# A bias that comes to all partitions by DMA instead of GpSimd's broadcast, a first weight load as a step of its own, and a new order of steps

## The chip, the cores and the metric

The kernel runs on one core of a Trainium2 chip. The metric is device microseconds of one execution; the median of several runs counts. The profile is one further execution, taken by the hardware profiler.

## The reference

Attention with rotary embedding over 4 batches, 8 heads, 576 positions and a head dimension of 64, then two layers of mixture of experts over the 2304 tokens of 512 elements. In the first layer a bias is added to the routing logits by the token's modality; the change touches how this bias gets to the chip.

```python
attn = softmax(rotate(q) @ rotate(k).T / sqrt(64)) @ v        # per batch and head
x = attn as [2304, 512]
# first layer: 8 experts, each token goes to one
logits = x @ w_gate + modality_bias[modality_id]              # [2304, 8]
e = argmax(logits); g = softmax(logits)[e]
x = g * (relu(x @ w1[e]) @ w2[e])
# second layer: only tokens with x @ w_skip > 0
x = x + g2 * (relu(x @ w1_2[e2]) @ w2_2[e2])
```

## The kernel before

**The attention** goes over 16 pairs of heads (p = 0 to 15, four pairs to a batch). Each pair is cut into some 100 small steps, which are Python functions in `attention` (L268 to L681): `load` (q, k, v by SP), `rope0` and `rope1` (the rotation of q and of k, L321; VectorE for the first pair, GpSimd for the others), `qk_tr`, `qk_hi`, `qk_lo` (transposition on TensorE into PSUM, and the split into a high and a low part on ScalarE and VectorE), `stackq`, `stackk`, `stack2` (ten moves from SBUF to SBUF by SP's queue, L401 to L423, that put the parts into the layouts that the score matmuls want), `s_mm`, `s_max`, `s_exp` (scores, maximum, exponential), `t_mm`, `t_hi`, `t_lo` (transposes of the exponentials), `pv` (the product with v, whose split is `v_hi` on ScalarE and `v_lo` on GpSimd), `o_ev`, `o_mm`, `o_norm` (output transposition L577, division by the sums, and the routing logits), and `x_store` (L586: three DMAs, of 256 KB and twice 16 KB, of the pair's output to the output tensor).

`s_mm0a` to `s_mm3b` take the scores of 128 rows each; `s_mm4` takes the last 64 rows of both heads. The "a" half reads what `stackq` and `stackk` move, `s_mm4` also what `stack2` moves.

**The order** is written out by hand. Every step has a place in the table POS; pair p's step stands at 10 * p + POS, steps outside the pairs stand at base 0, 110 (what follows the twelfth pair) or 150. All steps are sorted by place, and each engine and each DMA queue gets its instructions in that order (L609 to L681). So only the order between steps of one engine matters, not the numbers themselves. Engines wait for each other by semaphores.

**Around the change.** `constants1` (L223) has SP load small tables, among them the bias as one row of 16 numbers in `mbr`. `constants2` (L236) has GpSimd spread it over 128 partitions with `partition_broadcast` into `mbb`, and convert the modality ids. `constants3` (VectorE) and `constants4` (GpSimd) make `bias1` from it, which `route1` adds to the logits of a batch. `constants6` (L259) has SP load the second gate and fill the two lists in DRAM with void entries (L265). `route1` to `route4p` are the routing of a batch, mostly on GpSimd; `scat0` to `scat4` are indirect DMAs that write token numbers into the list (L807). After the twelfth pair `ahead1` counts tokens of three batches and picks the first expert, `ahead2` has SP load that expert's w1 into `raw1` (L1018, four pieces of 512 KB) and GpSimd load the first two parts of the list (L947), and `ahead3` makes token numbers of them (L1042) and gathers their rows (L951). `moe1_load2` loads w2 into `raw2`, which shares its memory with rope's tiles (`mem_w`). `x_mm0` and `x_mm1` (L1073) transpose the gathered rows, `m_mm` (L1094) multiplies with w1. `warm1` to `warm3` are dummy transposes (L600).

The expert layers behind the attention take blocks of 256 and of 128 tokens in a list order that the data decide; nothing in them is edited.

Of the kernel before, what the change touches and what calls it, by code (L numbers as in the profile page):

```python
# [10 lines left out]
F32 = mybir.dt.float32  # L11
# [11 lines left out]
N, DM, E, F = 2304, 512, 8, 1024  # L23
# [13 lines left out]


POS = dict(
    load=-36.7017, rope0=-33.9451, rope1=-30.111, v_hi=-21.4821, v_lo=-18.1897,  # L40
    qk_tr0=(-30.6061, -30.6042, -30.5936, -30.1223), qk_tr1=(-28.4904, -28.4904, -28.4848, -28.4848),
    qk_tr2=(-29.2463, -29.2463), qk_hi0=-29.4052, qk_hi1=-27.2491, qk_hi2=-29.202, qk_lo0=-29.1934, qk_lo1=-26.9027,
    qk_lo2=-28.9941, stackq=-25.8754, stackk=-23.011, stack2=-22.5711,
    s_mm0a=(-22.0577, -22.0577, -22.0577, -22.0577), s_max0a=-21.4825, s_exp0a=-20.8972,
    s_mm1a=(-21.3076, -21.3076, -21.3076, -21.3076), s_max1a=-20.1346, s_exp1a=-19.5976,
    s_mm2a=(-22.2316, -22.2316, -22.2316, -22.2316), s_max2a=-21.7162, s_exp2a=-21.4126,
    s_mm3a=(-20.5225, -20.5225, -20.5225, -20.5225), s_max3a=-19.2489, s_exp3a=-17.295,
    s_mm0b=(-14.3536, -14.1043, -14.0042, -13.9921), s_max0b=-12.9587, s_exp0b=-12.9046,
    s_mm1b=(-13.0069, -12.9105, -12.9105, -12.9105), s_max1b=-12.8704, s_exp1b=-12.8563,
    s_mm2b=(-15.4526, -15.4526, -15.4386, -15.4386), s_max2b=-14.6158, s_exp2b=-14.0784,  # L50
    s_mm3b=(-16.5055, -16.5055, -16.5055, -16.5055), s_max3b=-15.336, s_exp3b=-15.2119,
    s_mm4=(-19.1859, -19.1807, -19.1807, -19.1807, -19.1807, -19.1807, -19.1807, -19.1331), s_max4=-17.2632,
    s_exp4=-16.1016, l_mma=(-12.7178, -12.6968, -12.6968, -12.6968, -12.6968), l_hia=-12.6823, l_loa=-12.3966,
    t_mm0a=(-12.9092, -12.9092, -12.9092, -12.9092), t_hi0a=-12.8887, t_lo0a=-12.6464,
    pv0a=(-12.6813, -12.3155, -12.1921, -12.051), t_mm1a=(-14.662, -14.3587, -14.3361, -14.0627), t_hi1a=-14.0257,
    t_lo1a=-12.9105, pv1a=(-11.482, -10.94, -10.9025, -10.9025), t_mm2a=(-16.3817, -16.3207, -16.3207, -16.3207),
    t_hi2a=-15.4958, t_lo2a=-15.2606, pv2a=(-12.0718, -11.7295, -11.7295, -11.7295),
    t_mm3a=(-16.0635, -15.4829, -15.3061, -15.3061), t_hi3a=-14.423, t_lo3a=-14.3448,
    pv3a=(-11.6779, -11.4985, -11.4827, -11.4827), pv4a=(-10.0997, -9.6192), o_eva=-8.4242,
    o_mma=(-3.8821, -3.1843, -3.04, -3.0069, -3.0069), o_norma=-2.9092,  # L60
    l_mmb=(-12.5752, -12.5752, -12.5752, -12.5752, -12.5752), l_hib=-12.3276, l_lob=-12.2073,
    t_mm0b=(-12.4134, -12.3969, -12.3818, -12.3818), t_hi0b=-12.2316, t_lo0b=-11.9973,
    pv0b=(-6.7017, -6.7017, -6.7017, -6.5129), t_mm1b=(-7.8953, -7.8953, -7.8953, -7.4024), t_hi1b=-6.7199,
    t_lo1b=-6.1978, pv1b=(-5.2632, -4.5696, -3.9061, -3.5847), t_mm2b=(-11.6405, -11.6405, -11.6405, -11.6405),
    t_hi2b=-11.3076, t_lo2b=-11.3076, pv2b=(-6.5077, -6.5077, -6.2903, -6.172),
    t_mm3b=(-10.8705, -10.8705, -10.8705, -10.8705), t_hi3b=-9.8594, t_lo3b=-9.5279,
    pv3b=(-5.2659, -5.2659, -5.2659, -5.2659), pv4b=(-3.1789, -3.0274), o_evb=-3.008,
    o_mmb=(-2.908, -2.9041, -2.9041, -2.8421, -2.8421), o_normb=-2.5794,
    t_mm4=(-12.3715, -12.3715, -12.3715, -12.3715), t_hi4=-11.4863, t_lo4=-11.4473, r_inv=-4.0473, x_store=-1.9435,
    route1=-0.138, route2=22.2105, route2a=0.0711, route2b=2.3991, route2c=5.809, route2d=6.9931, route2e=3.0369,  # L70
    route2p=7.9451, route3=10.8285, route4=11.1643, route4p=13.5564, scat0=15.9086, scat1=17.0957, scat2=21.6619,
    scat3=22.8497, scat4=24.3127, ahead1=20.7865, ahead2=24.8061, ahead3=26.173, load2=-9.6073, w_hi0=-4.399,
    w_lo0=-2.8576, w_hi1=-10.8843, w_lo1=-10.3037, w_hi2=-3.048, w_lo2=429.3001, w_hi3=-3.3916, w_lo3=-3.1985,
    x_mm0=-2.5275, x_hi0=-2.4128, x_lo0=-2.2031, x_mm1=-2.35, x_hi1=-2.1246, x_lo1=-2.0387, m_mm0=48.2393,
    m_hi0=181.3328, m_lo0=1552.441, m_mm1=611.0564, m_hi1=1628.6892, m_lo1=1629.4085, m_mm2=1553.3863, m_hi2=1625.391,
    m_lo2=1629.4891, m_mm3=6.3202, m_hi3=25.9681, m_lo3=44.977, route1z=0.3768, route2z=49.5846, route2pz=83.0433,
    route3z=164.2886, route4z=197.8744, route4pz=247.5439, scat0z=1554.3317, scat1z=1556.1501, scat2z=1556.8609,
    scat3z=1626.076, scat4z=1629.4488, w2_hi0=3.7676, w2_lo0=6.9592, w2_hi1=0.3352, w2_lo1=2.9321, w2_hi2=-0.7596,
# [34 lines left out]
class Kernel:  # L113
# [154 lines left out]
    def attention(self):  # L268

        nc, wp, pp, rp = self.nc, self.wp, self.pp, self.rp  # L270
# [353 lines left out]
        for p in range(NPAIR):  # L624
# [903 lines left out]
```

## Time and profile before

| | us |
|---|---|
| median of three runs (769.36 to 770.71) | 769.93 |
| profiled execution, its own time | 767.88 |
| its span, from first to last instruction | 766.2 |
| TensorE busy | 725.8 (95%) |
| VectorE, ScalarE, GpSimd busy | 504.0, 435.3, 359.4 |

The mean granted clock of TensorE is 0.975 of full speed. Full speed is 2.4 GHz; the other level is 1.2 GHz. The profiled execution's own time lies 2.05 us below the median of the runs, and its span 1.68 us below its own time.

In the rows, PE is TensorE, DVE VectorE, ACT ScalarE, POOL GpSimd, SP the engine that issues most DMAs; a q behind the name is the engine's sequencer. An arrow names what ended a wait.

### The profile page before, as it was taken

How to read it: one execution, taken by the hardware profiler on the slowest of the kernel's cores; microseconds unless marked ns; L12 is line 12 of the kernel's file. 1: busy time of each engine (PE TensorE's matmuls, PEld its weight loads, DVE VectorE, ACT ScalarE, POOL GpSimd, SP SyncE). 2: the span in 40 equal slices, each digit the busy share in tenths (PEclk: the TensorE clock that was granted, in tenths of full speed). 3: DMA queues.
4: the chain of work that ended last, by engine and by line, in shares of the span. 5: the costliest groups of instructions: out<-in, count | busy, mean ns of one | idle time of the engine just before them, and what ended most of it. 6: DMA issues, size and time to landing. Idle time of an engine off the chain costs nothing. (4 is left out here: it accounts for less than half of the span.)

```text
span 766.2 us, 15348 instructions
## 1 busy us (share of the span) xinstructions
PE 725.8 (95%) x4948; PEld 654.8 (85%) x4948; DVE 504.0 (66%) x1216; ACT 435.3 (57%) x940; POOL 359.4 (47%) x498
## 2 busy tenths in 40 slices
PE   7898999999999999979899999999999979999994
PEld 6797999999999999968799989988998868877773
DVE  6786899988898899984433333323446753589892
ACT  3785888888888888871222222222235542388781
POOL 7728548767876785253343323231434512133233
PEclk8898999999999999999999999999999989999998
DMA  4654554655465544460011101211693301669910
GB/s 139 137 136 121 136 131 120 148 134 134 119 149 131 137 118 102 118 221 1 15 57 42 42 29 49 51 33 38 178 338 146 124 6 40 242 247 316 325 48 20
DMA packets 75199, 92.29 MB, mean 120 GB/s; under 512 B 29440, under 2 KB 50176, under 8 KB 75090
## 3 DMA queue, kind: packets, MB, share of 16 engines
q1 hardware_dynamic: 65938, 73.74, 34.4%
q0 software_dynamic: 7200, 12.46, 5.2%
q10 hardware_dynamic: 1952, 4.85, 2.1%
q8 instruction: 43, 0.70, 0.4%
q14 instruction: 66, 0.54, 0.3%
HBM read 62.11 MB, written 12.95 MB: 98 GB/s over the span
## 5 line engine op out<-in xcount | busy, mean ns | idle before, releaser
L430 PE MATMUL S<-w1s 128*128 128x288 f32 x640 | 124.8, 321 | 3.0 <-DVE w1s L398 1.2
L1143 PE MATMUL psY<-w2s,hT 128*128 128x512 f32 x480 | 119.3, 397 | 0.0
L1094 PE MATMUL psM<-xT,w1s 128*128 128x256 f32 x864 | 112.6, 287 | 0.0
L1094 PEld LDWEIGHTS psM<-xT,w1s 128*128 128x128 f32 x864 | 106.8, 191 | 0.6 <-issue 0.6
L430 PEld LDWEIGHTS S<-w1s 128*128 128x128 f32 x640 | 95.9, 195 | 6.7 <-ACT PP L447 1.6
L1143 PEld LDWEIGHTS psY<-w2s,hT 128*128 128x128 f32 x480 | 87.2, 188 | 16.7
L447 ACT ACTIVATE PP<-S,nm 128x576 f32<-128x576 f32 x128 | 95.8, 748 | 8.0 <-DVE nm L443 7.5
L443 DVE TENSOR_REDUCE nm<-S 128x1 f32<-128x576 f32 x128 | 94.7, 750 | 3.4 <-PE S L430 3.4
L532 DVE TENSOR_TENSOR tl<-T,th 128x512 fp32r<-128x512 f32 x128 | 88.0, 687 | 11.8 <-ACT th L528 8.7
L525 PE MATMUL T<-ident,PP 128*128 128x128 f32 x512 | 87.4, 275 | 1.1 <-DVE w1s L399 0.4
L528 ACT CAST th<-T 128x512 fp32r<-128x512 f32 x128 | 74.8, 584 | 17.5 <-PE T L525 14.9
L559 PE MATMUL O<-th,vh 128*128 128x288 f32 x256 | 74.0, 329 | 0.6 <-ACT os L568 0.5
L1107 DVE SCALAR_TENSOR_TENSOR hT<-psM,hT 128x512 fp32r<-128x512 f32 x36 | 24.9, 690 | 68.6 <-ACT hT L1102 57.8
L1407 PE MATMUL psY<-w2s,hT 128*128 128x512 f32 x240 | 63.8, 403 | 4.3 <-DVE hT L1386 4.3
L1367 PE MATMUL psM<-w1s,xT 128*128 128x512 f32 x240 | 62.4, 408 | 4.5 <-DVEq L1290 4.5
L525 PEld LDWEIGHTS T<-ident,PP 128*128 128x128 f32 x512 | 63.1, 141 | 3.6 <-DVE tl L532 0.8
L1102 ACT ACTIVATE hT<-psM 128x512 fp32r<-128x512 f32 x36 | 21.5, 598 | 74.1 <-PE psM L1094 73.6
L559 PE MATMUL O<-tl,vh 128*128 128x288 f32 x256 | 61.7, 306 | 0.0
L961 POOL DMA_INDIRECT list<-tg,si x20 | 20.2, 1008 | 85.7 <-issue 56.2
L1367 PEld LDWEIGHTS psM<-w1s,xT 128*128 128x128 f32 x240 | 45.0, 193 | 14.7 <-ACTq L1290 4.6
L1407 PEld LDWEIGHTS psY<-w2s,hT 128*128 128x128 f32 x240 | 43.0, 188 | 15.3 <-DVE hT L1386 6.9
L330 POOL TENSOR_TENSOR mem_w<-qkn,mem_w 128x640 f32<-128x640 f32 x30 | 47.0, 1568 | 19.1 <-PE T L367 11.9
(263 smaller groups left out, 1413.9 us busy)
## 6 DMA issues: line engine op xcount, KB each, us to landing
raw<-in_moe_w_dram SPq DMA_DIRECT2D x20, 512.0 KB
mem_w<-in_moe_w_dram SPq DMA_DIRECT2D x20, 512.0 KB
w1s<-w1s SPq DMA_DIRECT2D x30, 256.0 KB
raw1b<-in_moe_w_dram SPq DMA_DIRECT2D x12, 512.0 KB
raw2b<-in_moe_w_dram SPq DMA_DIRECT2D x12, 512.0 KB
w1s<-w1s SPq DMA_DIRECT2D x16, 288.0 KB
qkn<-in_q_dram SPq DMA_DIRECT2D x16, 256.0 KB
qkn<-in_k_dram SPq DMA_DIRECT2D x16, 256.0 KB
```

The source lines that it names most:

```text
L330: eng.tensor_tensor(r, x, tb[:, i, 0].unsqueeze(1).broadcast_to([128, 2, 5, D]), op=ALU.mult)
L430: yield nc.tensor.matmul(ps[:, hf, 0:288], s["wide"][:, o : o + 128], s["K"][h % 2][:, kk, hf * 288 : hf * 288 + 288], start=first and kk ...
L443: nc.vector.tensor_reduce(st[h // 2]["nm"][:, h % 2, c : c + 1], hs[h]["ps", c][:, :, 0:288], axis=AX.XY, op=ALU.max, negate=True)
L447: nc.scalar.activation(PP[:, c, h % 2 * S : h % 2 * S + S].rearrange("p (a b) -> p a b", a=2), hs[h]["ps", c][:, :, 0:288], AF.Exp, bias=s ...
L525: yield nc.tensor.transpose(ps[:, c * 128 : c * 128 + 128], PP[:, c, o : o + 128], ident)
L528: nc.scalar.copy(hs[h]["th"][:, j, 0:512], hs[h]["tp", j])
L532: nc.vector.tensor_tensor(s["tl"][:, j, 0:512], s["tp", j], s["th"][:, j, 0:512].bitcast(F32), op=ALU.subtract)
L559: yield nc.tensor.matmul(s["ot"][:, hf, 0:288], st[h // 2]["vh"][:, h % 2, j].rearrange("p s d -> p (s d)"), w[:, hf * 288 : hf * 288 + 28 ...
L1094: self.nc.tensor.matmul(ps[:, a], self.w1s[:, wi, dc, fs], x[:, xi, dc], start=(dc == 0 and wi + xi == 0), stop=(dc == 3 and wi == 1))
L1143: nc.tensor.matmul(ps, h[:, hi, f, t * 128 : t * 128 + 128], w2s[:, wi, f], start=(f == 0 and hi + wi == 0), stop=(f == 7 and hi == 1))
L1367: nc.tensor.matmul(ms[hf], x[:, xi, dc], w1s[:, wi, dc, hf * 512 : hf * 512 + 512], start=(dc == 0 and wi + xi == 0), stop=(dc == 3 and xi ...
L1407: nc.tensor.matmul(y, hT[:, hi, f], w2s[:, wi, f], start=(f == 0 and hi + wi == 0), stop=(f == 7 and hi == 1))
```

## The change

The bias is loaded into all 128 partitions by the DMA that brought one row before, and the broadcast goes. The load of the first expert's w1 is taken out of `ahead2` and gets a place of its own. All places in POS are new; most of a pair's steps move by about 7 together, which changes nothing between them. Of the table only the lines with steps that are spoken of below stand here.

```diff
-    load=-36.7017, rope0=-33.9451, rope1=-30.111, v_hi=-21.4821, v_lo=-18.1897,
+    load=-40.2545, rope0=-39.1031, rope1=-38.1966, v_hi=-28.3147, v_lo=-23.8684,
...
-    qk_lo2=-28.9941, stackq=-25.8754, stackk=-23.011, stack2=-22.5711,
+    qk_lo2=-35.4693, stackq=-30.1381, stackk=-30.0982, stack2=-25.509,
...
-    t_mm4=(-12.3715, -12.3715, -12.3715, -12.3715), t_hi4=-11.4863, t_lo4=-11.4473, r_inv=-4.0473, x_store=-1.9435,
-    route1=-0.138, route2=22.2105, route2a=0.0711, route2b=2.3991, route2c=5.809, route2d=6.9931, route2e=3.0369,
+    t_mm4=(-19.6242, -19.6242, -19.6242, -19.6242), t_hi4=-18.9706, t_lo4=-17.4754, r_inv=-11.2088, x_store=1.9574,
+    route1=-6.9814, route2=22.2105, route2a=-4.1901, route2b=-1.229, route2c=0.1453, route2d=4.0619, route2e=-0.6407,
...
-    scat3=22.8497, scat4=24.3127, ahead1=20.7865, ahead2=24.8061, ahead3=26.173, load2=-9.6073, w_hi0=-4.399,
+    scat3=16.9444, scat4=19.5742, ahead1=14.2223, ahead2=19.7233, ahead3=29.4759, load1=14.5742, load2=-24.2645,
...
-    x_mm0=-2.5275, x_hi0=-2.4128, x_lo0=-2.2031, x_mm1=-2.35, x_hi1=-2.1246, x_lo1=-2.0387, m_mm0=48.2393,
+    w_lo3=-10.9597, x_mm0=-8.6121, x_hi0=-8.4037, x_lo0=-8.2937, x_mm1=-9.9397, x_hi1=-8.6978, x_lo1=-8.5079,
...
-    w2_hi6=5.4516, w2_lo6=35.4726, w2_hi7=-0.1195, w2_lo7=1.6545, const1=-11.4827, const6=-0.4859, const2=-2.0544,
-    const3=21.5765, const4=22.9241, const5=-41.9989, warm1=-42.8466, warm2=-28.4242, warm3=-36.7926, warm4=1629.4689,
+    w2_hi5=-6.1284, w2_lo5=11.6538, w2_hi6=-9.6901, w2_lo6=-8.8372, w2_hi7=-10.1036, w2_lo7=11.0842, const1=-19.7718,
+    const6=29.8505, const2=-1.1138, const3=13.7753, const4=21.8754, const5=-41.303, warm1=-41.3244, warm2=-27.378,
...
-        self.mbr = self.wp.tile([1, 2, E], F32, name="mbr", bufs=1)
-        nc.sync.dma_start(self.mbr, self.mb.unsqueeze(0))
+        self.mbb = self.wp.tile([128, 2, E], F32, name="mbb", bufs=1)
+        nc.sync.dma_start(self.mbb, self.mb.unsqueeze(0).broadcast_to([128, 2, E]))
...
     def constants2(self):
 
         nc, cp = self.nc, self.cp
-        self.mbb = self.wp.tile([128, 2, E], F32, name="mbb", bufs=1)
-        nc.gpsimd.partition_broadcast(self.mbb, self.mbr)
         self.mf = self.wp.tile([128, B * 5], F32, name="mf", bufs=1)
...
                 for i, f in enumerate((self.moe1_ahead1, self.moe1_ahead2, self.moe1_ahead3)):
                     at(10 * p, f"ahead{i + 1}", f)
+                at(10 * p, "load1", self.moe1_load1)
...
-    def moe1_ahead2(self):
+    def moe1_load1(self):
         q = self.q1
         q.e = self.reg(q.first["meta"][0:1, 0:1], [ET.SP], E - 1)
         self.load(self.raw1, q.w[0], q.e)
+
+    def moe1_ahead2(self):
+        q = self.q1
         for i in range(NA1):
             self.seq_list(q, i)
```

What the sorted table gives for each queue, where it differs:

- SP before: load, stackq, stackk, stack2, x_store (of two pairs back) and again. After: load, stackq, stackk, x_store (of three pairs back), stack2. constants6 stood between the first x_store and the fifth load; it now stands between the eighth load and the seventh pair's stackq. constants1 now stands ahead of the second pair's stack2. At the end, before: the stores of the 13th and 14th pair, w1, the 15th pair's store, w2, the last store; after: the 13th pair's store, w1, w2, the last three stores.
- GpSimd before: rope0 of the fourth pair, constants2, rope1, v_lo; after: rope0, rope1, v_lo, constants2. rope1 now comes ahead of route1 and of route2d.
- TensorE: warm2 stood ahead of the first score matmuls s_mm2a of the first pair and now stands behind s_mm1a, ahead of s_mm3a. x_mm1 comes ahead of x_mm0. Some transposes and matmuls of a pair change places.
- VectorE and ScalarE: the order within a pair stays; small routing steps and the order of the weight splits at the end change.

## Rows read from the trace of the kernel before

**Rows 1.** Windows: busy us (count) of each engine, clock, DMA share, GB/s.
```profile
60.00:80.00 20.00, 16.22 (x111) 15.56 (x111) 11.97 (x27) 11.46 (x29) 14.88 (x13) 0.83 0.46 113
80.00:100.00 20.00, 20.00 (x161) 19.05 (x160) 18.00 (x36) 17.23 (x41) 11.10 (x9) 1.00 0.54 135
```

**Rows 2.** TensorE's timeline in the attention: start us, us, what, idle time before.
```profile
42.33 0.60 PE L364 MATMUL T<-ident,mem_w 128*128 128x128 f32 x4
...
48.10 0.34 PE L577 MATMUL T<-IIg,os 128*128 128x72 f32 x2
...
64.07 0.37 PE L367 MATMUL T<-ident,mem_w 64*128 64x64 f32 x1 [3.78 <-POOL mem_w L336]
...
73.80 0.34 PE L577 MATMUL T<-IIg,os 128*128 128x72 f32 x2
...
150.44 0.34 PE L577 MATMUL T<-IIg,os 128*128 128x72 f32 x2
...
181.73 1.32 PE L430 MATMUL S<-w1s 128*128 128x288 f32 x8
```

**Rows 3.** GpSimd's timeline around constants2.
```profile
44.56 1.57 POOL L336 TENSOR_TENSOR mem_w<-mem_w 128x640 f32<-128x640 f32 x1
51.94 0.29 POOL L240 PARTITION_BROADCAST mbb<-mbr  x1 [5.81 <-issue]
...
59.23 1.54 POOL L330 TENSOR_TENSOR mem_w<-qkn,mem_w 128x640 f32<-128x640 f32 x1 [6.84 <-PE T L525]
```

**Rows 4.** Instructions of lines 240 and 330: ns min/median/max, first to last start.
```profile
L240 POOLq MODIFY_POOL_CONFIG  x2: 15/15/15, 46.1 to 46.1; - x2
...
L330 POOLq MODIFY_POOL_CONFIG  x2: 102/102/102, 52.3 to 52.4; - x2
```

**Rows 5.** SP's timeline: constants6's void stores, and one steady pair.
```profile
55.67 1.96 SPq L265 DMA_DIRECT2D list<-void  x2
...
163.92 9.93 SPq L402 DMA_DIRECT2D w1s<-w1s  x10
...
174.60 2.28 SPq L592 DMA_DIRECT2D out_dram<-xb  x2
```

**Rows 6.** TensorE's timeline at the start.
```profile
14.59 1.35 PE L600 MATMUL O<-ident 128*128 128x128 f32 x8
...
21.81 0.84 PE L364 MATMUL T<-ident,mem_w 128*128 128x128 f32 x3
22.30 1.31 PE L430 MATMUL S<-w1s 128*128 128x288 f32 x4
```

**Rows 7.** SP's timeline: the first expert's w1 and w2.
```profile
318.78 2.34 SPq L1018 DMA_DIRECT2D raw<-in_moe_w_dram  x4
...
330.67 2.20 SPq L1018 DMA_DIRECT2D mem_w<-in_moe_w_dram  x4
```

**Rows 8.** GpSimd's timeline at the hand-over.
```profile
319.30 0.93 POOL L807 DMA_INDIRECT list<-g_tg,g_si  x1 [2.93 <-DVE nm L464]
326.49 0.79 POOL L947 DMA_DIRECT2D list<-list  x1 [6.27 <-DMA list<-g_tg,g_si]
...
330.50 0.18 POOL L1042 CAST tok<-list 128x2 int32<-128x2 f32 x1 [2.30 <-DMA list<-list]
...
332.78 1.48 POOL L951 DMA_INDIRECT xg<-out_dram,tok  x1 [0.30 <-issue]
```

**Rows 9.** TensorE's timeline at the hand-over.
```profile
341.32 0.63 PE L1073 MATMUL T<-ident,xg 128*128 128x128 f32 x4 [1.45 <-DMA xg<-out_dram,tok]
...
343.35 7.17 PE L1094 MATMUL S<-xT,w1s 128*128 128x256 f32 x47 [0.32 <-DVE xT L1080]
...
352.09 3.12 PE L1094 MATMUL S<-xT,w1s 128*128 128x256 f32 x24
```

**Rows 10.** Windows: two us beside the first load (columns as in rows 1).
```profile
324.00:326.00 2.00, 2.00 (x20) 2.00 (x18) 1.62 (x4) 1.83 (x4) 0.00 (x0) 1.00 1.04 414
```

**Rows 11.** DMA issues: out<-in, queue, count, median us to landing.
```profile
xg<-out_dram,tok POOLq DMA_INDIRECT x22, 4.0
```

More of the change, by code (lines that the diff above doesn't have):

```diff
@@ L39 @@
 POS = dict(
-    load=-36.7017, rope0=-33.9451, rope1=-30.111, v_hi=-21.4821, v_lo=-18.1897,
-    qk_tr0=(-30.6061, -30.6042, -30.5936, -30.1223), qk_tr1=(-28.4904, -28.4904, -28.4848, -28.4848),
-    qk_tr2=(-29.2463, -29.2463), qk_hi0=-29.4052, qk_hi1=-27.2491, qk_hi2=-29.202, qk_lo0=-29.1934, qk_lo1=-26.9027,
-    qk_lo2=-28.9941, stackq=-25.8754, stackk=-23.011, stack2=-22.5711,
-    s_mm0a=(-22.0577, -22.0577, -22.0577, -22.0577), s_max0a=-21.4825, s_exp0a=-20.8972,
-    s_mm1a=(-21.3076, -21.3076, -21.3076, -21.3076), s_max1a=-20.1346, s_exp1a=-19.5976,
@@ L46 @@
[L46 to L68, printed above, removed]
@@ L69 @@
-    t_mm4=(-12.3715, -12.3715, -12.3715, -12.3715), t_hi4=-11.4863, t_lo4=-11.4473, r_inv=-4.0473, x_store=-1.9435,
-    route1=-0.138, route2=22.2105, route2a=0.0711, route2b=2.3991, route2c=5.809, route2d=6.9931, route2e=3.0369,
-    route2p=7.9451, route3=10.8285, route4=11.1643, route4p=13.5564, scat0=15.9086, scat1=17.0957, scat2=21.6619,
-    scat3=22.8497, scat4=24.3127, ahead1=20.7865, ahead2=24.8061, ahead3=26.173, load2=-9.6073, w_hi0=-4.399,
-    w_lo0=-2.8576, w_hi1=-10.8843, w_lo1=-10.3037, w_hi2=-3.048, w_lo2=429.3001, w_hi3=-3.3916, w_lo3=-3.1985,
@@ L74 @@
-    x_mm0=-2.5275, x_hi0=-2.4128, x_lo0=-2.2031, x_mm1=-2.35, x_hi1=-2.1246, x_lo1=-2.0387, m_mm0=48.2393,
[L75 to L78, printed above, removed]
@@ L79 @@
-    w2_lo2=-0.5096, w2_hi3=-2.8008, w2_lo3=-0.4501, w2_hi4=4.8596, w2_lo4=46.894, w2_hi5=-2.8731, w2_lo5=-2.4756,
-    w2_hi6=5.4516, w2_lo6=35.4726, w2_hi7=-0.1195, w2_lo7=1.6545, const1=-11.4827, const6=-0.4859, const2=-2.0544,
-    const3=21.5765, const4=22.9241, const5=-41.9989, warm1=-42.8466, warm2=-28.4242, warm3=-36.7926, warm4=1629.4689,
-    switch=-2.9023,
+    load=-40.2545, rope0=-39.1031, rope1=-38.1966, v_hi=-28.3147, v_lo=-23.8684,
+    qk_tr0=(-36.4818, -36.4818, -36.4175, -36.417), qk_tr1=(-35.1706, -35.1663, -35.1663, -35.1663),
@@ new lines @@
+    qk_tr2=(-35.5703, -35.5703), qk_hi0=-35.957, qk_hi1=-34.3626, qk_hi2=-35.507, qk_lo0=-35.509, qk_lo1=-34.3303,
+    qk_lo2=-35.4693, stackq=-30.1381, stackk=-30.0982, stack2=-25.509,
+    s_mm0a=(-29.1183, -29.1183, -28.9408, -28.9408), s_max0a=-27.5667, s_exp0a=-27.1082,
+    s_mm1a=(-27.658, -27.4021, -27.3816, -27.3816), s_max1a=-26.9413, s_exp1a=-26.9313,
+    s_mm2a=(-29.2907, -29.2907, -29.2907, -29.2907), s_max2a=-28.5991, s_exp2a=-28.0836,
+    s_mm3a=(-27.0942, -27.0942, -27.0896, -26.5376), s_max3a=-25.7889, s_exp3a=-24.5167,
@@ new lines @@
+    s_mm0b=(-21.3933, -21.3218, -21.2364, -21.1351), s_max0b=-20.8898, s_exp0b=-20.1501,
+    s_mm1b=(-20.265, -20.265, -20.265, -20.265), s_max1b=-20.0834, s_exp1b=-20.0491,
+    s_mm2b=(-23.1397, -22.8759, -22.4974, -21.9517), s_max2b=-21.7647, s_exp2b=-21.2057,
+    s_mm3b=(-23.6054, -23.6054, -23.6054, -23.6054), s_max3b=-22.8573, s_exp3b=-21.7306,
+    s_mm4=(-25.509, -25.509, -25.509, -25.509, -25.509, -25.509, -25.509, -25.509), s_max4=-24.5095, s_exp4=-23.3429,
+    l_mma=(-19.9277, -19.8564, -19.8547, -19.8547, -19.8547), l_hia=-19.7903, l_loa=-19.5979,
@@ new lines @@
+    t_mm0a=(-20.2584, -20.2584, -20.2584, -20.2584), t_hi0a=-20.1435, t_lo0a=-19.8475,
+    pv0a=(-19.7532, -19.5386, -19.5386, -19.0661), t_mm1a=(-21.4037, -21.3931, -21.308, -21.1784), t_hi1a=-21.0926,
+    t_lo1a=-20.3081, pv1a=(-17.4208, -17.4208, -17.4208, -17.4208), t_mm2a=(-23.5987, -23.5987, -23.5987, -23.5987),
+    t_hi2a=-22.9611, t_lo2a=-21.9235, pv2a=(-18.5945, -18.5377, -18.5377, -18.4638),
+    t_mm3a=(-23.1562, -22.9715, -22.7639, -21.8633), t_hi3a=-21.4737, t_lo3a=-21.2216,
+    pv3a=(-18.1424, -18.1045, -18.1045, -18.1045), pv4a=(-16.4217, -15.8968), o_eva=-14.5228,
@@ new lines @@
+    o_mma=(-11.0449, -10.4623, -10.3177, -10.2721, -10.2721), o_norma=-10.149,
+    l_mmb=(-19.8547, -19.8547, -19.8463, -19.8463, -19.8463), l_hib=-19.7903, l_lob=-19.2907,
+    t_mm0b=(-19.7903, -19.7903, -19.7903, -19.7903), t_hi0b=-19.3042, t_lo0b=-19.0191,
+    pv0b=(-14.2645, -14.2611, -14.2184, -13.7614), t_mm1b=(-14.2645, -14.2645, -14.2645, -14.2645), t_hi1b=-14.2645,
+    t_lo1b=-13.6402, pv1b=(-11.4085, -11.255, -11.188, -10.8691), t_mm2b=(-18.1246, -18.0426, -18.0426, -18.0426),
+    t_hi2b=-17.8371, t_lo2b=-17.2765, pv2b=(-13.9306, -13.7514, -13.4001, -13.4001),
@@ new lines @@
+    t_mm3b=(-17.2287, -17.2145, -17.2145, -17.2145), t_hi3b=-17.0935, t_lo3b=-15.7978,
+    pv3b=(-13.2291, -11.7069, -11.7069, -11.7069), pv4b=(-10.4564, -10.2754), o_evb=-10.2431,
+    o_mmb=(-10.0879, -10.0879, -10.0879, -10.0879, -10.0879), o_normb=-9.6242,
+    t_mm4=(-19.6242, -19.6242, -19.6242, -19.6242), t_hi4=-18.9706, t_lo4=-17.4754, r_inv=-11.2088, x_store=1.9574,
+    route1=-6.9814, route2=22.2105, route2a=-4.1901, route2b=-1.229, route2c=0.1453, route2d=4.0619, route2e=-0.6407,
+    route2p=4.5019, route3=4.5974, route4=5.2785, route4p=8.5911, scat0=8.6015, scat1=11.1598, scat2=15.9148,
@@ new lines @@
+    scat3=16.9444, scat4=19.5742, ahead1=14.2223, ahead2=19.7233, ahead3=29.4759, load1=14.5742, load2=-24.2645,
+    w_hi0=-18.0218, w_lo0=-12.5724, w_hi1=-10.4271, w_lo1=14.5241, w_hi2=-10.9172, w_lo2=89.3681, w_hi3=-11.6986,
+    w_lo3=-10.9597, x_mm0=-8.6121, x_hi0=-8.4037, x_lo0=-8.2937, x_mm1=-9.9397, x_hi1=-8.6978, x_lo1=-8.5079,
+    m_mm0=-7.4459, m_hi0=10.9118, m_lo0=88.8036, m_mm1=82.5617, m_hi1=88.8547, m_lo1=2082.5947, m_mm2=2078.0174,
+    m_hi2=2080.779, m_lo2=2082.2001, m_mm3=-7.478, m_hi3=-4.5908, m_lo3=11.7616, route1z=-7.6683, route2z=13.1714,
@@ new lines @@
+    route2pz=14.2751, route3z=18.1897, route4z=18.276, route4pz=88.7524, scat0z=89.1618, scat1z=2080.5695,
+    scat2z=2080.6514, scat3z=2080.7351, scat4z=2080.771, w2_hi0=-6.9032, w2_lo0=11.369, w2_hi1=-8.0059,
+    w2_lo1=-6.3604, w2_hi2=-8.8296, w2_lo2=-7.5691, w2_hi3=-10.1245, w2_lo3=-10.0138, w2_hi4=-7.4619, w2_lo4=-4.7776,
+    w2_hi5=-6.1284, w2_lo5=11.6538, w2_hi6=-9.6901, w2_lo6=-8.8372, w2_hi7=-10.1036, w2_lo7=11.0842, const1=-19.7718,
+    const6=29.8505, const2=-1.1138, const3=13.7753, const4=21.8754, const5=-41.303, warm1=-41.3244, warm2=-27.378,
@@ L83 @@
+    warm3=-41.014, warm4=2082.9893, switch=-10.1407,
 )
```

## The prediction

> **What bounds the kernel now.** The profiled execution's own time is 767.88 us (table above); the median of the three timed runs is 769.93 us (769.36 to 770.71). What I take off the one I take off the other. A measurement of this kernel tells some 0.2%, 1.5 us, from no change.
>
> I read the windows first. In the stretch from 80 us on TensorE is busy 20.00 of 20.00 us at a granted clock of 1.00, and up to 300 us the stretches look alike. The one before it stands out: from 60 to 80 us TensorE worked 16.22 us at a mean clock of 0.83 [rows 1]. So in the attention only what makes TensorE wait counts; what the other engines and the queues do beside it is free while its slack lasts.
>
> Next comes TensorE's timeline. Each pair of heads has a first output transposition (L577 x2). From the second pair's, at 73.80, to the sixth's, at 150.44, four pairs took 76.64 us, 19.16 us each. From the first pair's, at 48.10, to the second's it was 25.70 us [rows 2]: this one pair is **6.54 us** too long. The transposition L367 at 64.07 waited 3.78 us of that for GpSimd's rope (mem_w L336), and behind this idle time the clock fell: 0.83 as a mean over 20 us is seven of them at 1.2 GHz, which takes the other 3 us.
>
> GpSimd's timeline says why rope was late. Between the fourth pair's rope0, whose last piece (44.56) ends at 46.13, and its rope1, which starts at 59.23, stands constants2: the partition_broadcast starts at 51.94 after 5.81 us put down to "issue", and after it another 6.84 us pass [rows 3]. Ahead of each gap stand two MODIFY_POOL_CONFIG instructions, of L240 at 46.1 and of L330 at 52.3 [rows 4]: the engine is set up for the broadcast and set back for the next tensor_tensor. The profile puts the second gap down to TensorE's L525; but of TensorE rope1 needs only that the third pair's transposes have read its tile, and those (L364 x4 at 42.33) ended at 42.93 [rows 2].
>
> **The broadcast.** Removed are the broadcast and both changes of setup, 59.23 - 46.13 = 13.1 us of GpSimd with a short copy that stays. Added on SP are only more, shorter pieces in a DMA that was there already, and constants4 reads it only pairs later. Rope1 then starts at 46.1 and ends near 51, not at 64, and TensorE asks for it at 60.3 (64.07 less 3.78). Nothing else is late at this place: rope1 and v_lo now even stand ahead of constants2, and x_store and constants6 no longer stand ahead of the next load on SP. The pair becomes one like the others: **-6.5**. Ends: -6.0 with half a us of waits left, -6.7.
>
> **The order in the steady pairs.** VectorE and ScalarE keep their order but for the small route steps; TensorE's steps move by at most about 1 us within a pair, and none is added. Cost 0; a transposition between two score matmuls instead of ahead of them might cost or give 0.05 us, in 14 pairs 0.7 either way.
>
> On SP, x_store now stands between stackk and stack2. Its DMAs hold SP for 3.0 us (173.85, where the ten moves end, to 174.60 + 2.28 = 176.88) [rows 5]; it waits for nothing there, since its o_norm lies far back. Queued behind it are stack2's two moves, and for these TensorE's eight s_mm4 wait: at 181.73 [rows 2], 7.9 us after the moves' end. 3.0 us later leaves 4.9 for landing: 0; without this cover each us would cost every pair one. The load behind starts no later, as x_store no longer waits for o_norm just ahead of it.
>
> Constants6 (its larger part, two void stores, took 1.96 us of SP [rows 5]) moves from ahead of the fifth load to behind the eighth, ahead of the seventh pair's stackq. There SP sat waiting until v_lo freed a buffer; v_lo comes sooner, since route1 and constants4's wait for VectorE shrink. 0, at most 1 us once. Constants1 ahead of the second pair's stack2 shifts that by under 4 us; its s_mm4 has such slack, as above: 0. GpSimd does rope1 ahead of route1 and route2d, which gives rope room; the routing has half a pair before route3 asks: 0.
>
> **The start.** warm2, eight dummy transposes, took 1.35 us at 14.59, while TensorE had to wait anyway. It now stands behind s_mm1a, ahead of s_mm3a, which began at 22.30 behind three transposes from 21.81 [rows 6]. Here TensorE is slow and paces the others. 21.81 + 1.35 = 23.16 is 0.9 us later than 22.30: **+0.9**. Ends: 0 if ScalarE's later waits swallow it, +1.4 in full.
>
> **The hand-over to the experts.** ahead1 keeps its place, so the first load starts as before, its issue ending at 318.78 + 2.34 = 321.1. But load2 follows at once on SP, not at 330.67 [rows 7], and the stores of the 14th and 15th pair queue behind both; only the third block's gather reads these, long after. What decides is GpSimd's chain on its own queue: the last scatter into the list (319.30), the list loads (326.49), the token copy (330.50), the gathers (the second at 332.78) [rows 8], and TensorE's second x transposition at 341.32 [rows 9]. The scatter before the load's traffic held up its follower for 2.93 us (the row names VectorE, which has no part in the list), the one beside it for 6.27 [rows 8]: traffic costs 3.3 us. The list loads, now beside load2, so bring the copy to 333.8 at worst. Both loads are 4.2 MB, 10.1 us at the 414 GB/s of [rows 10], from 321.1 on: drained at 331.2, or 332.5 at a mean rate below that. I take 333.3 for the copy. The second gather follows 2.28 us later, at 335.6, and lands after 4.0 us [rows 11], at 339.6: 1.7 us ahead of 341.32, and both transpositions follow at once, as x_mm1 now comes first. The 47 matmuls behind took 7.17 us where 48 at full clock take 6.2 (24 in 3.12) [rows 9]; part of that us may come back. Against it stands that the first transposition starts later than its 339.25. I take **-1.5**; ends: -3.3 (list loads not delayed, clock kept) and +1.0 (list loads held until load2 is drained, 2.5 us more). The moved splits of w1 and w2 end beside route3z, which waits for GpSimd: 0.
>
> The Trainium skill's page "DMA: Bandwidth & Descriptors", section "Queues, rings and completion order", says that each DMA engine takes turns between the queues packet by packet, so that a short transfer would hardly be held up by a long one on another queue. By it the list loads would lose almost nothing and the sum would be 1.8 us lower. The 6.27 us against 2.93 speak against most of that.
>
> **Sum.** -6.5 + 0.9 - 1.5 = -7.1: the profiled execution at 760.8, the median at **762.8**. The expert blocks behind have no edit and only start earlier.
>
> **Rivals.** First, the second gap is no change of setup but a true wait for TensorE's L525, as the releaser column has it. Then rope1 starts near 58.6, 0.6 us sooner than now, and the pair stays long: 769.93 - 0.6 + 0.9 - 1.5 = 768.7. For it speaks that column; against it L364's end at 42.93 and the MODIFY_POOL_CONFIG ahead of the gap: 0.04. The Trainium skill's page "GPSIMD Engine Reference", section "Instruction dispatch", gives about 6 us, without an instruction that shows, to the first call after such a change. The first gap, 5.81, agrees; the second is longer.
>
> Second, slower: stack2 comes too late for s_mm4 in every pair. It decides from the 7.9 us less the landing, about 5 us of delay; the issue alone is 3.0. If x_store's transfers go ahead as well and the last move comes 6 us late, TensorE loses 1.1 us in each of 14 pairs: 762.8 + 15.4 = 778.2. Against it: the store's bytes (256 KB and two times 16) move in about a us: 0.04.
>
> Third, load2 holds back the list loads until it is drained: +1.0 in place of -1.5, 765.3; 0.10.
>
> Fourth, the queues take turns: the list loads lose nothing, the second gather lands by 337, x waits for TensorE and not the reverse, and the clock stays: -3.3 in place of -1.5, 761.0; 0.10. The Trainium skill's rule quoted above is this one.
>
> That the change doesn't do what it says gets no share: the broadcast is the one instruction of GpSimd that is set up in mid-kernel.
>
> **Numbers.** My forecast has 0.72; the third and fourth rival are faster too. Faster by over 0.2% (below 768.4): 0.72 + 0.10 + 0.10 = 0.92; within: 0.04; slower: 0.04. All good ends (-6.7, -0.7, 0, -3.3) give 759.2, all bad ones (-6.0, +0.7, +1.4, +1.0) 767.0; as all the bad ones hardly meet, I take 759.3 to 766.3, which leaves out the first two rivals.
>
> **What would show it.** Right: no MODIFY_POOL_CONFIG and no gap on GpSimd near 46 us; 19.2 us from every pair's L577 to the next; the second x transposition one to three us closer behind the last L577. Wrong: a wait of TensorE for mem_w, or for w1s in each pair; list loads that land later than on the old scale's 334; s_mm3a later by over 1.5 us; L577 more than 19.3 us apart.

## The result and the profile after

The kernel after takes 762.34 us (median of six runs, 759.27 to 763.86) where the kernel before took 770.11 beside it: a ratio of 0.9898, with a 95% interval of 0.9878 to 0.9918. That is 7.8 us less (6.3 to 9.4). The profiled execution took 761.60 us, its span is 760.0. Of all executions below, one is left out of its kernel's ratio: b_pad22's longest, 1009.14 us at a mean granted clock of 0.65.

The windows of after that answer to [rows 1]: TensorE's clock is 1.00 in both, where it was 0.83 in the first.

```profile
60.00:80.00 20.00, 19.88 (x161) 19.06 (x159) 18.11 (x37) 17.86 (x42) 11.10 (x9) 1.00 0.59 141
80.00:100.00 20.00, 19.78 (x159) 19.09 (x159) 18.31 (x39) 17.87 (x45) 11.61 (x10) 1.00 0.56 131
```

TensorE's timeline of after, for [rows 2]: the output transposition is now L575. From the first pair's to the second's it is 19.01 us, not 25.70, and no wait for `mem_w` is left.

```profile
49.37 0.34 PE L575 MATMUL T<-IIg,os 128*128 128x72 f32 x2
...
68.38 0.34 PE L575 MATMUL T<-IIg,os 128*128 128x72 f32 x2
...
144.50 0.34 PE L575 MATMUL T<-IIg,os 128*128 128x72 f32 x2
```

GpSimd's timeline of after, for [rows 3]: rope1 of the fourth pair (47.33) follows rope0 without a gap, the copy that is left of constants2 stands behind v_lo, and no MODIFY_POOL_CONFIG of these lines [rows 4] is in the trace.

```profile
45.82 1.55 POOL L334 TENSOR_TENSOR mem_w<-mem_w 128x640 f32<-128x640 f32 x1
47.33 1.55 POOL L328 TENSOR_TENSOR mem_w<-qkn,mem_w 128x640 f32<-128x640 f32 x1
...
57.16 1.57 POOL L345 TENSOR_TENSOR vh<-vn,vh 128x640 fp32r<-128x640 f32 x1 [4.98 <-ACT vh L340]
58.67 0.20 POOL L240 CAST mf<-mi 128x20 f32<-128x20 int32 x1
```

Cut at the same instructions of TensorE, the two profiled executions divide so (the first matmul of w2 is L1143, now L1145; that of the second layer L1367, now L1369):

| stretch, us | before | after | difference |
|---|---|---|---|
| up to TensorE's first instruction | 1.70 | 1.48 | -0.22 |
| to the first pair's output transposition | 46.40 | 47.89 | +1.49 |
| to the second pair's | 25.70 | 19.01 | -6.69 |
| to the 16th pair's (14 pairs) | 261.80 | 260.30 | -1.50 |
| to the first matmul of w2 | 24.89 | 25.84 | +0.95 |
| to the second expert layer | 261.31 | 261.22 | -0.09 |
| to the end | 144.43 | 144.21 | -0.22 |

So the large term is there, and four smaller things need a cause: the start, a shorter period, a hand-over that gains nothing in this execution, and an expert part that is as long as before although one late stretch at half clock is gone from it (24 matmuls of L1094 behind the first oh took 4.61 us, those of L1096 now 3.06; b_dma, in the old order, has 3.10, so this is not the new order's).

### The profile page after: what moved, and what is told of

It is laid out like the page before. It is cut to its first block, busy times and chain, and to the rows that moved or that the text cites. A ratio compares the mean times of both kernels' runs of the same rounds, so it can differ in the third digit from the quotient of the medians.

```text
span 760.0 us, 15381 instructions
## 1 busy us (share of the span) xinstructions
PE 718.9 (95%) x4948; PEld 652.8 (86%) x4948; DVE 504.1 (66%) x1216; ACT 441.8 (58%) x940; POOL 360.6 (47%) x497
## 5 line engine op out<-in xcount | busy, mean ns | idle before, releaser
L428 PE MATMUL S<-w1s 128*128 128x288 f32 x640 | 134.1, 323 | 4.0 <-ACT w1s L384 1.3
L1145 PE MATMUL psY<-w2s,hT 128*128 128x512 f32 x480 | 119.4, 397 | 0.0
L1096 PE MATMUL psM<-xT,w1s 128*128 128x256 f32 x864 | 110.9, 285 | 0.0
L428 PEld LDWEIGHTS S<-w1s 128*128 128x128 f32 x640 | 98.7, 192 | 8.8 <-ACT PP L445 1.7
L1096 PEld LDWEIGHTS psM<-xT,w1s 128*128 128x128 f32 x864 | 105.2, 189 | 0.6 <-issue 0.6
L1145 PEld LDWEIGHTS psY<-w2s,hT 128*128 128x128 f32 x480 | 87.2, 188 | 16.8
L523 PE MATMUL T<-ident,PP 128*128 128x128 f32 x512 | 94.3, 274 | 0.8 <-DVE w1s L397 0.4
L557 PE MATMUL O<-th,vh 128*128 128x288 f32 x256 | 76.4, 331 | 0.9 <-ACT os L566 0.9
L1369 PE MATMUL psM<-w1s,xT 128*128 128x512 f32 x240 | 62.0, 406 | 6.3 <-DVEq L1292 6.3
L557 PE MATMUL O<-tl,vh 128*128 128x288 f32 x256 | 64.4, 305 | 0.0
L1369 PEld LDWEIGHTS psM<-w1s,xT 128*128 128x128 f32 x240 | 44.7, 192 | 16.5 <-issue 6.4
```

The lines of the kernel that those rows point to most:

```text
L428: yield nc.tensor.matmul(ps[:, hf, 0:288], s["wide"][:, o : o + 128], s["K"][h % 2][:, kk, hf * 288 : hf * 288 + 288], start=first and kk ...
L523: yield nc.tensor.transpose(ps[:, c * 128 : c * 128 + 128], PP[:, c, o : o + 128], ident)
L557: yield nc.tensor.matmul(s["ot"][:, hf, 0:288], st[h // 2]["vh"][:, h % 2, j].rearrange("p s d -> p (s d)"), w[:, hf * 288 : hf * 288 + 28 ...
L1096: self.nc.tensor.matmul(ps[:, a], self.w1s[:, wi, dc, fs], x[:, xi, dc], start=(dc == 0 and wi + xi == 0), stop=(dc == 3 and wi == 1))
L1145: nc.tensor.matmul(ps, h[:, hi, f, t * 128 : t * 128 + 128], w2s[:, wi, f], start=(f == 0 and hi + wi == 0), stop=(f == 7 and hi == 1))
L1369: nc.tensor.matmul(ms[hf], x[:, xi, dc], w1s[:, wi, dc, hf * 512 : hf * 512 + 512], start=(dc == 0 and wi + xi == 0), stop=(dc == 3 and xi ...
```

## The experiments

**The broadcast alone.** The kernel before gets the two lines of the bias (the mbr lines become mbb with `broadcast_to`, the `partition_broadcast` goes) and nothing else.

> The kernel before with the bias DMA alone, every step in its old place. My theory (the 13.1 us of GpSimd around the broadcast are two changes of its setup, and rope1 waits for nothing else): no gap on GpSimd between rope0 and rope1 of the fourth pair, 19.1 to 19.2 us from the first to the second L577 in place of 25.70, no MODIFY_POOL_CONFIG of L240 or L330, and the median 6.5 us under before (763.6 beside 770.1). Rival (the second gap is a true wait for TensorE): the distance stays at 25.1, the median at 769.5.

Measured: 0.9914 of before (0.9888 to 0.9941), 6.6 us less than 767.51. The distance is 19.13 us; GpSimd goes from rope0 through the copy to rope1 without a gap:

```profile
44.82 1.55 POOL L334 TENSOR_TENSOR mem_w<-mem_w 128x640 f32<-128x640 f32 x1
46.32 0.20 POOL L240 CAST mf<-mi 128x20 f32<-128x20 int32 x1
46.49 1.58 POOL L328 TENSOR_TENSOR mem_w<-qkn,mem_w 128x640 f32<-128x640 f32 x1
```

**Twice the broadcast,** to see what its price hangs on:

```diff
         nc.gpsimd.partition_broadcast(self.mbb, self.mbr)
+        nc.gpsimd.partition_broadcast(self.mbb, self.mbr)
```

> The kernel before with the partition_broadcast called twice, one behind the other. My theory (each gap is one change of GpSimd's setup, the call itself takes 0.3 us): the gaps stay one each (5.8 and 6.8 us), rope1 starts 0.3 us later, 26.0 us from the first L577 to the second in place of 25.7, the median 0.3 over before. Rival (each call brings its own 6 us): a third gap, 32 us from the first L577 to the second, the median 6 over before.

Measured: 1.0006 of before (0.9988 to 1.0024), 25.95 us from L578 to L578. The second call comes 0.38 us behind the first; the gaps stay two:

```profile
52.38 0.29 POOL L240 PARTITION_BROADCAST mbb<-mbr  x1 [5.48 <-issue]
52.76 0.29 POOL L241 PARTITION_BROADCAST mbb<-mbr  x1
52.91 0.28 POOL L243 CAST mf<-mi 128x20 f32<-128x20 int32 x1
60.02 1.54 POOL L331 TENSOR_TENSOR mem_w<-qkn,mem_w 128x640 f32<-128x640 f32 x1 [6.83 <-PE T L526]
```

The price is that of going to the other kind of instruction and back, once each, not that of the call. The cast right behind the call (52.91) has no gap ahead of it: the way back is paid only ahead of the next tensor_tensor (60.02).

**The broadcast in the new order:** after, with `mbr` and the `partition_broadcast` back in constants2.

> The kernel after with the row mbr and the partition_broadcast put back into constants2, which now stands behind the third pair's v_lo on GpSimd. If the cost belongs to the broadcast wherever it stands: 6.5 us more than after (768.8), in the next pair instead. If it belongs to its place ahead of rope1 (my reading of the slack): GpSimd's gaps of 5.8 and 6.8 us begin at 58.7, the fifth pair's rope0 starts at 71.8 and not at 61.5, its rope1 ends at 81.5, and TensorE, which asks for the 64-column transposes at 80.2, waits 1.3 us: 763.6 in all, 1.3 more than after, so that most of what the DMA gave could have been had by the order alone.

Measured: 0.9946 (0.9927 to 0.9965), by the ratios 3.8 us more than after. GpSimd's gaps are 5.87 and 7.45 us, TensorE's wait at 82.91 is 1.76 us, and behind it 84 to 88 us stand at a granted clock of 0.57, so that this pair takes 22.56 us. Neither expectation held: the place hides nearly half of the price, but I had priced the wait alone and not the clock behind it.

```profile
82.91 0.27 PE L367 MATMUL T<-ident,mem_w 64*128 64x64 f32 x1 [1.76 <-POOL mem_w L336]
...
84.00:88.00 4.00, 4.00 (x22) 4.00 (x21) 2.14 (x3) 2.73 (x7) 3.92 (x5) 0.57 0.30 86
```

**The start.** After, with `warm2` at -29.2908 in place of -27.378, ahead of the first s_mm2a again.

> The kernel after with warm2 in its old place ahead of the first s_mm2a. My theory (the eight dummy transposes of 1.55 us stand in TensorE's way at half clock): s_mm3a follows the last s_mm1a 1.0 us sooner, the first L575 comes at 48.1 and not 49.37, the median 1.0 to 1.3 under after. Rival (ScalarE and VectorE pace the start; warm2 fills a wait): the first L575 within 0.3 us of 49.37.

Measured: 0.9883 (0.9858 to 0.9908), the first L575 at 48.13. The interval overlaps that of after, and the start differs between executions, so the profiles decide: in the seven with warm2 behind s_mm1a the first output transposition comes at 49.20 to 50.86, in the two with the new table and warm2 in its old place (this one and best_pad42) at 48.13 and 48.34. In after warm2 stood at 21.59 and held s_mm3a until 23.14; here s_mm1a and s_mm3a run through (20.39), and warm2 lies in a wait (14.30):

```profile
21.59 1.91 PE L598 MATMUL O<-ident 128*128 128x128 f32 x8
23.14 1.31 PE L428 MATMUL S<-w1s 128*128 128x288 f32 x4
```

```profile
14.30 1.42 PE L598 MATMUL O<-ident 128*128 128x128 f32 x8
...
20.39 2.29 PE L428 MATMUL S<-w1s 128*128 128x288 f32 x8 [0.81 <-ACT PP L445]
```

**The period.** In the steady pairs of before one product of P with v (`pv0a`'s first, L559) stands between the two groups of L505/L508 transposes; in after it stands behind them. Two kernels move it alone: back in the new table, and out in the old one (with the bias DMA). Of each line of the table only the entry that changes stands here.

```diff
-    pv0a=(-19.7532, -19.5386, -19.5386, -19.0661)
-    l_mmb=(-19.8547, -19.8547, -19.8463, -19.8463, -19.8463)
+    pv0a=(-19.8532, -19.5386, -19.5386, -19.0661)
+    l_mmb=(-19.8530, -19.8530, -19.8463, -19.8463, -19.8463)
```

> The kernel after with pv0a's first pair of matmuls back between l_mma and l_mmb on TensorE, as before (between the two groups of transposes of the 64-row part). My theory (before, this one matmul group between two groups of transposes cost TensorE 0.48 us from group to group where it now costs 0.24): 0.12 to 0.24 us more per pair, 19.1 to 19.25 from L575 to L575, the median 1.7 to 3.4 over after. Rival (the 0.12 us per pair came from the 0.3 us ahead of the q transposition L364, or from x_store's new place): 18.99 stays, the median as after.

Measured: 0.9963 (0.9944 to 0.9982), 4.7 us over after beside it (764.52 and 759.84). The period is 19.28 us in place of 19.00, a little over the 19.25 that I gave at most; over the 14 pairs that is 4.1 us (264.39 and 260.33), and 1.5 us more lie in the hand-over (21.36 and 19.88, below). The place of the difference, first in this kernel, then in after: from the first L503 to the L557 behind L536 it is 2.07 us with the product in the middle and 1.84 without.

```profile
149.95 0.46 PE L503 MATMUL S<-ident,P 64*128 64x64 f32 x4
150.24 0.22 PE L506 MATMUL S<-ident,P 64*128 64x64 f32 x1
150.40 0.40 PE L557 MATMUL O<-th,vh 128*128 128x288 f32 x1
150.73 0.46 PE L503 MATMUL S<-ident,P 64*128 64x64 f32 x4
...
152.02 0.38 PE L557 MATMUL O<-th,vh 128*128 128x288 f32 x1
```

```profile
148.15 0.46 PE L503 MATMUL S<-ident,P 64*128 64x64 f32 x4
148.45 0.22 PE L506 MATMUL S<-ident,P 64*128 64x64 f32 x1
148.55 0.46 PE L503 MATMUL S<-ident,P 64*128 64x64 f32 x4
...
149.99 0.38 PE L557 MATMUL O<-th,vh 128*128 128x288 f32 x1
```

```diff
-    pv0a=(-12.6813, -12.3155, -12.1921, -12.051)
+    pv0a=(-12.3750, -12.3155, -12.1921, -12.051)
```

> The kernel before with the bias DMA, and with pv0a's first pair of matmuls moved out from between the two groups of l_mm transposes, behind t_mm0b, as the new table has it; all else in the old order. Putting that pair back into the new table cost 0.28 us per pair. If the same holds in the old table: 19.13 less 0.28 = 18.85 us from L575 to L575, 0.14 less than after, 14 pairs and the first: 4 us under the kernel with the DMA alone (0.9914 to about 0.986 of before). If the gain needs the other new places too: 19.0 to 19.13.

Measured: 0.9885 (0.9859 to 0.9911), the period 18.97 us. Against the 19.13 of the DMA alone that is 0.16, not 0.28: a wait of 0.16 us ahead of the q transposition L362 takes part of it back. Neither expectation held to the number, but one step moved makes the old order as short as the new one.

**The hand-over.** After, with load2 behind the 15th pair's store (-7.9) and the first w2 splits behind x's.

> The kernel after with load2 (w2) behind the 15th pair's store on SP, as before, and the first w2 splits behind the splits of x. My theory (the list loads were held up by w2's traffic, 5.06 us against 2.30): the token copy L1041 follows the second list load by some 2.5 us and starts near 324.5 in place of 326.98; the x transposes follow the last L575 without a wait for xg (0.98 us now), so x comes 0.9 us sooner; w2's splits still end well ahead of the first L1145, the median 0 to 1 us under after. Rival (the lists' 5 us are their own): copy and x where they are, the median as after or worse by late splits.

Measured: 0.9913 (0.9889 to 0.9936); after beside the next kernels has 0.9897, so nothing is gained. The token copy came at 321.29, but not because the list loads were faster: the copy waited 4.55 us for them without w2, and 5.06, 3.71 and 4.11 us with it (after, after again, a_warm). My theory fell. The third rival falls too: in a_warm the list is there at 319.97, when the queues had moved some 2.1 MB since 314 us, half of the two loads, and they go on moving some 380 GB/s.

```profile
319.97 0.18 POOL L1041 CAST tok<-list 128x2 int32<-128x2 f32 x1 [4.11 <-DMA list<-list]
...
324.00:326.00 2.00, 1.08 (x9) 1.09 (x9) 0.69 (x1) 1.07 (x3) 1.70 (x2) 1.00 1.07 388
326.00:328.00 2.00, 2.00 (x19) 2.00 (x17) 1.59 (x2) 2.00 (x3) 0.15 (x1) 1.00 1.08 368
```

The same kernel after once more:

> The kernel after, unchanged, beside the next three, to see what its hand-over and its expert part do a second time. If the 4.41 to 6.31 us behind the branch at the end of the first expert layer belong to the program: 6.2 us again, as in the three other kernels with the new table, and 4.49 only with the old table. If they are chance: anything between. The attention: first L575 at 49.2 to 49.4, 18.99 us from pair to pair. Ratio to before 0.990.

Measured: 0.9897 (0.9876 to 0.9918). The wait at the branch (below) is 6.17 us again. The first L575 came at 50.86, outside my 49.2 to 49.4: the start differs by up to 1.5 us between executions of one kernel. And the hand-over is another one. In the first profile of after (the first three rows; its list loads, issued at 320.21, had waited 7.26 us for the last scatter) x waits for the gathers, and the first matmuls of w1 run partly at half clock (0.83 from 334 to 344 us). In the second (the last three rows) x waits for no gather:

```profile
333.35 1.06 PE L1075 MATMUL T<-ident,xg 128*128 128x128 f32 x8 [0.98 <-DMA xg<-out_dram,tok]
...
335.98 7.31 PE L1096 MATMUL S<-xT,w1s 128*128 128x256 f32 x47 [0.45 <-DVE xT L1082]
...
345.15 0.18 PE L779 MATMUL T<-acc,ones 128*128 128x40 bf16 x1 [1.83 <-POOL acc L761]
```

```profile
333.74 0.60 PE L1075 MATMUL T<-ident,xg 128*128 128x128 f32 x4
334.64 0.63 PE L1075 MATMUL T<-ident,xg 128*128 128x128 f32 x4 [0.30 <-PE T L1075]
...
336.67 5.90 PE L1096 MATMUL S<-xT,w1s 128*128 128x256 f32 x47 [0.34 <-DVE xT L1082]
```

From the end of the last L575 to the first matmul of w2 before took 21.55 us (b_dma 21.54, b_two 21.70, b_dma_pv0 21.09, b_pad22 24.18), after 22.15 and the second time 19.88; a_bcast, a_warm, a_load2, a_pad10 and best_pad42 have 19.8 to 20.0, a_pv0 21.36, a_wlo1 (next) 18.56. So 1.7 us are what most profiles gain, six of nine in the new order, and the profile I first saw was an exception. To the first matmul of w1 it is 3.69 us in before, 2.77 in after and 2.05 the second time: the 1.7 us are x, which comes sooner. Where the half clock falls differs: in the first 47 matmuls of w1 (before 7.17 us), in the 48 behind acc (7.49 in after the second time, 6.15 in a_wlo1), in both (after, a_pv0) or in neither (a_load2, a_wlo1).

In the rows above TensorE waits 1.83 us for acc, in before 0.91: beside acc VectorE now splits w1 (`w_lo1`).

```profile
342.99 1.22 DVE L985 TENSOR_TENSOR w1s<-raw,w1s 128x1024 fp32r<-128x1024 f32 x1
...
343.15 2.23 POOL L761 TENSOR_TENSOR acc<-acc,g_oh 128x8 bf16<-128x8 bf16 x5 [3.15 <-DVE g_oh L753]
```

After, with `w_lo1=11.7`, ahead of m_lo3:

> The kernel after with w_lo1 (one split of w1 on VectorE, 128x1024, 1.22 us) ahead of m_lo3 and not behind route2z. My theory (VectorE and GpSimd slow each other: acc L761 took 2.23 us beside this split where it took 1.31 before): acc takes 1.3 us again, TensorE's wait for it falls from 1.83 to 0.91, the second 48 matmuls of m_mm start 0.9 us sooner, the median 0.9 under after. Rival (acc's length has nothing to do with the split): 1.83 stays, 0.

Measured: acc takes 1.31 us and TensorE's wait is 0.91, as expected. The median is 0.9892 (0.9871 to 0.9912), against 0.9897: a gain of 0.9 us is too small to be told here, and later TensorE waits 2.06 us for the first oh and runs the 24 matmuls behind it in 4.60 us, in the second profile of after 0.72 and 3.10.

```profile
342.62 1.31 POOL L761 TENSOR_TENSOR acc<-acc,g_oh 128x8 bf16<-128x8 bf16 x5 [5.41 <-DVE g_oh L753]
...
343.70 0.18 PE L779 MATMUL T<-acc,ones 128*128 128x40 bf16 x1 [0.91 <-POOL acc L761]
```

The Trainium skill, page "SBUF — State Buffer", section "Who interferes with whom", says that a VectorE instruction with two inputs in SBUF contends with a GpSimd instruction that reads SBUF. The split is such a one, and acc's 2.23 us beside it against 1.31 without it agree.

**The branch.** At the end of the first expert layer all engines take a branch (L1290, now L1292). TensorE's first matmul behind it waited 4.49 us with the old table and 5.98 to 6.35 in seven profiles with the new one. Counted in the trace, VectorE has 1,280 instructions ahead of it with the old table and 1,302 with the new, 22 waits on semaphores more. Three kernels add dummy instructions to VectorE where it is idle:

```diff
+        at(150, "pad", lambda: [nc.vector.memset(self.padt, 0.0) for _ in range(10)])
```

> The kernel after with ten dummy memsets of 128x1 on VectorE behind w_lo2, where VectorE has nothing to do. VectorE stood 2.92 us behind the branch of line 1290 with the old table and 4.3 to 4.5 us behind the same branch with the new one, with 22 instructions more ahead of it. If that is where the code lies in memory: ten more (32 in all) can move the 4.4 to another value, and TensorE's wait there from 6.2 towards 4.5; elsewhere nothing changes. If it is what the code waits for: 6.0 to 6.4 again.

> The kernel before with 22 dummy memsets of 128x1 on VectorE behind w_lo2, as many instructions as the new table has more ahead of the branch at the end of the first expert layer. If the place of VectorE's code decides: VectorE stands some 4.3 us behind that branch and not 2.92, TensorE waits 6.0 to 6.4 us and not 4.49, the median 1.7 over before (1.002). If the new table's longer wait has to do with what its instructions are: 2.92 and 4.49 stay, the median as before.

> The kernel after with warm2 in its old place, w_lo1 ahead of m_lo3, and 42 dummy memsets on VectorE behind w_lo2 (64 instructions more than with the old table). The two moves: 1.2 and 0.9 us, so 0.987 of before where after has 0.990. The wait at the branch: 4.5 in place of 6.2 if the place of the code decides and 64 suits it as the old place did, 1.7 us more of gain; 6.2 if not.

Measured: first TensorE's matmul in before; then VectorE's branch and its next instruction (first and last start of two each) and TensorE's matmul in after and in a_pad10 (1,312 instructions); then TensorE's matmul alone in b_pad22 (1,302) and in best_pad42 (1,344).

```profile
621.80 0.77 PE L1367 MATMUL psM<-w1s,xT 128*128 128x512 f32 x1 [4.49 <-DVEq L1290]
```

```profile
L1292 DVEq COMPARE_BRANCH  x2: 47/52/56, 611.2 to 615.8; - x2
L1292 DVEq EVENT_SEMAPHORE  x2: 21/21/21, 615.6 to 615.7; - x2
615.74 0.77 PE L1369 MATMUL psM<-w1s,xT 128*128 128x512 f32 x1 [6.30 <-DVEq L1292]
```

```profile
L1294 DVEq COMPARE_BRANCH  x2: 47/52/56, 607.0 to 610.1; - x2
L1294 DVEq EVENT_SEMAPHORE  x2: 21/21/21, 609.9 to 610.0; - x2
610.09 0.77 PE L1371 MATMUL psM<-w1s,xT 128*128 128x512 f32 x1 [4.51 <-DVEq L1294]
```

```profile
621.50 0.77 PE L1369 MATMUL psM<-w1s,xT 128*128 128x512 f32 x1 [5.96 <-DVEq L1292]
```

```profile
608.85 1.49 PE L1371 MATMUL psM<-w1s,xT 128*128 128x512 f32 x3 [4.64 <-DVEq L1294]
```

Ten idle instructions take the wait from 6.2 to 4.51 us, 22 bring the kernel before from 4.49 to 5.96: what counts is how many instructions stand ahead of the branch on VectorE, whether they are semaphore waits or memsets. That this is a matter of where its code lies in memory is not shown. a_pad10 was run once, 755.64 us; b_pad22 has 1.0011 (0.9987 to 1.0036), which holds both the expected 1.002 and no change, so there the trace alone decides.

best_pad42 is the fastest kernel of the study, 0.9842 of before (0.9818 to 0.9867), 755.05 us: after, with warm2 in its old place, w_lo1 earlier, and the dummies. The three moves are not told apart in its median.

## Why the prediction was right, and where it was not

The time (762.8 against 762.34) and the first mechanism were right. Two terms were missing, of about the same size and of opposite sign (-1.5 in the steady pairs, +1.7 at the branch): that the sum came out within half a us is in part luck.

- **The broadcast, -6.5:** right. The DMA alone gives 25.70 - 19.13 = 6.57. The first rival, a true wait for TensorE, is out: rope1 starts at 46.49 in b_dma. That the DMA was needed for all of it is not so: the new order alone hides some 3 us.
- **The start, +0.9:** the mechanism right, the size short. s_mm3a came 1.06 us later against TensorE's first instruction, and taking warm2 back gave 1.24 in the trace. The rest of the 1.49 is mostly later waits for ScalarE (0.74 us ahead of the second L503 group, where before had 0.33). They come with the new place of pv0a's first product and not with warm2: a_warm and b_dma_pv0 have 0.74 too, a_pv0 has 0.33.
- **"The order in the steady pairs ... Cost 0":** the step that failed. I looked at transpositions between score matmuls and took a switch to cost or give 0.05 us at most; a single product between two groups of small transposes costs 0.23 us where it stands. Moving it alone takes 2.45 us off the 14 pairs of the old order (261.95 in b_dma, 259.50 in b_dma_pv0), more than the -1.50, so the other new places give some 0.9 us back; which ones, no run shows, nor why the product costs this much there.
- **x_store ahead of stack2, 0,** and the second rival: the profile lists no wait of TensorE from 50 to 300 us in after. Right, and so for constants1 and constants6.
- **The hand-over, -1.5:** right in most profiles (21.55 to 19.88, nearly all of it x that comes sooner, as I had it), not in the first one (+0.6 by the same count). My reason was partly wrong: the list loads are slow beside w1 as well as beside w2; b_dma's copy waited only 2.58 us, with its list loads issued at 318.01, when the queues moved 221 GB/s and less. And the 3.3 us that traffic costs the last scatter came from one row: the list loads behind it waited 3.3 to 7.3 us in the 14 profiles, not always 6.27. The third rival is refuted. The fourth, queues that take turns and cost the list nothing, is not what the rows show either (a wait of 3.7 to 5.4 us in ten profiles, 1.4 to 2.6 in the four whose list loads were issued at some 220 GB/s and less, among them the 2.30 of [rows 8]).
- **"The moved splits of w1 and w2 ... 0":** failed, 0.9 us on TensorE, for the w1 split beside acc.
- **"The expert blocks behind have no edit and only start earlier":** failed. They wait 1.7 us longer at a branch, because 22 more instructions (semaphore waits) stand ahead of it on VectorE.

With the usual hand-over the terms are -6.6 + 1.2 - 1.5 - 1.7 + 1.7 = -6.9; the medians say -7.8, and their interval (-9.4 to -6.3) holds it. What decides where a stretch at half clock falls in the hand-over stays open: a_pv0 and a_bcast had one in the first matmuls of w1 (47 in 7.38 us, not 5.90) with the same waits ahead of them as after the second time.

## What to carry to other kernels

A GpSimd instruction that the engine is set up for, as partition_broadcast here, is priced in mid-kernel by the change to its kind and back (5.5 to 7.5 us each way), so use none, or put it where the engine has slack for both ways, and add the clock that TensorE loses behind the wait. On an engine that is busy all the time, the order of its own instructions is a cost: compare start-to-start times over groups, not busy shares. Code behind a branch can move by 1.7 us when only the number of instructions ahead of it changes; look at the waits at branches of both kernels before one explains a small difference by the edit.

## What the runs showed of the hardware that I had not expected

VectorE's stop behind one and the same branch was 2.92 us with 1,280 instructions ahead, 2.93 with 1,312 and 3.06 with 1,344, but 4.06 to 4.45 with 1,302. The Trainium skill, page "Runtime: NRT & Kernel Launch", section "Instruction fetch mechanics", says that a branch to code outside what has been fetched makes the engine wait until a whole block of instructions is there. The dependence on the count agrees with it; the fetch itself is in no row here.

GpSimd's way back from the broadcast took longer (6.83 to 7.45 us) than the way there (5.48 to 5.87), in all four kernels that have it.
